# Masking the second batch on VectorE instead of TensorE, with an earlier table load, slots in three arrays and a planner that counts bank turns, in a fused attention and MoE kernel

## The chip, the cores and the metric

The kernel runs on one core of one Trainium2 chip. The metric is the device time of one execution in microseconds. A run's profile gives the span from the first to the last instruction; the time of the profiled execution is about 2 us more than its span.

## What is computed

Local attention with two kinds of masks, then a two-layer network with a leaky ReLU, all in fp32 at the interface:

```python
B, H, S, D = 8, 8, 576, 64
scores = q @ k.T / sqrt(D)
rel = pos[:, None] - pos[None, :]
mask_plain = (rel >= 0) & (rel < 32)                      # heads 0 to 3
mask_dil = (rel >= 0) & (rel < 128) & (rel % 4 == 0)      # heads 4 to 7
attn = softmax(where(mask, scores, -1e9))
x = (attn @ v).transpose(0, 2, 1, 3).reshape(B * S, H * D)   # 4608 x 512
h = x @ w_in                                              # 512 x 2048
out = maximum(0.01 * h, h) @ w_out                        # 2048 x 512
```

## The kernel before

**Attention.** The batches are taken one after another (`attend`). Each batch has four visits, in the order 2, 3, 0, 1; visits 2 and 3 are the dilated heads (`dil`), 0 and 1 the plain ones, two heads a visit, and each visit has two units. For a visit, q and k are cast to fp16 (`nat`), turned so that the head dimension lies across partitions, and stored with v in one of six slots, which lie side by side in one SBUF array `slots`: q, k and v of slot 0, then those of slot 1, and so on. For batches 0 and 1 (`b < EARLY`, EARLY = 2) the turning is done by TensorE into a PSUM bank (`tp`, and for batch 0 also others), from which VectorE or ScalarE copy into the slot (lines 398 and 400); the last 64 rows of q and k come by `load_rest` and `turn_rest` through the tile `rest`. Later batches are turned on VectorE.

A unit (`unit`) makes the scores of 384 or 416 columns with five matmuls in one PSUM bank (`p_bank`, line 775), takes exponentials on ScalarE into an fp16 tile `ee` (line 782), and then uses `ee` twice on TensorE: sums over keys (line 793 or 810), and products with v (line 793). ScalarE turns the sums into reciprocals by a logarithm and an exponential (lines 818 and 820, tile `rc`), and VectorE multiplies them into the products and writes `xt` (line 831).

Masking is done in two ways. For batches 0 and 1 (`by_pe`), two or three matmuls with the identity write a bias of 0 or -60000 into the bank ahead of the scores (line 771); the bias lies in the small part of the constants, loaded first. From batch 2 on, VectorE multiplies the exponentials in `ee` by a table of zeros and ones (line 786); the table is the large part of the constants, 400 KB.

**The network.** `up` multiplies `xt` by w_in into PSUM (lines 850 and 879), ScalarE applies the leaky ReLU on the way to `gt` (lines 865 and 891). For the first four output tiles `down` multiplies by w_out directly, in four parts of which the last needs the last pieces of w_out (line 916). Later tiles go in groups of four with seven block products in place of eight (line 1006), for which VectorE prepares sums (lines 946 and 992). The last three chunks use the same scheme for w_in (line 1275), with scratch memory in the slots that attention no longer needs.

**What sets the order.** Every piece of work is a task with candidate engines, an estimated cost, and dependencies. `_Plan` simulates the engines, chooses engine and order, repeats this nine times with priorities taken from the result, and keeps the shortest plan; the kernel is then issued in that order, one in-order queue to each engine. Margins (`MARGIN`) stretch the estimates of an engine after the planned time `CALM`. The loads of batches 0 and 1 and of the weights are in a fixed order, the list `FIRST`: q, v, r (the rest of q and k) with batch and head group, w0 to w7 for w_in, w8 to w15 for w_out, c for the table, and "." for a further piece of a v load. All of these but a few are issued from SyncE. The weights come as fp32 into tiles not yet used for anything else (`gt`, `wst`, `xt`), and VectorE and GpSimd cast them (line 387).

A rule of the framework adds semaphores where two engines use the same PSUM bank or overlapping memory.

Of the kernel before, what the change touches and what calls it, by code (L numbers as in the profile page):

```python
# [10 lines left out]
FP32 = mybir.dt.float32  # L11
# [41 lines left out]
class _Task:  # L53
    __slots__ = ("choices", "eng", "lat", "deps", "fn", "prio", "soft", "n", "start", "done",
                 "dur", "left", "ready", "users", "service", "kind", "late", "fixed", "rows", "yields")

    def __init__(self, choices, lat, deps, fn, prio, soft, n, kind):
# [10 lines left out]
        self.yields = []  # L68


class _Plan:
# [22 lines left out]
    def forward(self):  # L94
# [14 lines left out]
        cached = {}  # L109
        while len(order) < len(self.tasks):  # L110
            best = None
            for eng, cand in waiting.items():
# [4 lines left out]
                else:  # L117
# [10 lines left out]
                    for t in cand:  # L128
                        if len(t.choices) > 1:
                            end = max(here, t.ready) + dict(t.choices)[eng] * _margin(eng, here)  # L130
                            if any(max(free.get(e, 0.0), t.ready) + d * _margin(e, here) < end - 0.02
                                   for e, d in t.choices if e != eng):
                                continue
# [3 lines left out]
                    else:  # L137
                        at = max(here, min(t.ready for t in could))
                        pick = min(((t.ready + t.soft > at + 1e-9, t.prio, t.n), t)
                                   for t in could if t.ready <= at + 1e-9)  # L140
# [124 lines left out]
def kernel(  # L265
# [51 lines left out]
    KB, VB, TS = S, 3 * S, 5 * S  # L317
# [3 lines left out]
    slots = sbuf("slots", [128, NT * TS])  # L321
# [58 lines left out]
    def cast(dst, src, n, deps, prio, engines=("POOL", "DVE"), slow=1.0):  # L380
        cost = {"POOL": 0.15 + n * 0.00102 * slow, "DVE": 0.07 + n * (0.00055 if slow == 1.0 else 0.0011),
# [12 lines left out]
    def move(dst, src, n, deps, prio, eng=("DVE",), dense=False):  # L394
# [8 lines left out]
        return add(tuple((e, cost[e]) for e in eng), None, 0.2, deps, fn, prio)  # L403
# [18 lines left out]
    def clear_slots(which, prio, deps):  # L422
        for i in which:
            t_zero[i] = [clear((("DVE", 0.62), ("POOL", 0.7)),
                               slots[:, i * TS + x:i * TS + x + 2 * S].bitcast(FP32), None, 0.0,
                               prio + 0.01 * i, deps) for x in (KB, VB)]
# [6 lines left out]
    def slot(i, x, p0, p1, *dims):  # L433
        return at(slots, p0, p1, i * TS + x, *dims)
# [1023 lines left out]
```

## Time and profile before

| | us |
|---|---|
| median of 3 runs | 298.97 |
| lowest and highest | 298.3, 300.19 |
| profiled execution | 299.48 |
| its span | 297.5 |

The page's first part gives busy time by engine, the second the busy tenths in 40 slices of 7.4 us. PE is the matmuls and PEld the weight loads beside them; DVE is VectorE, ACT ScalarE, POOL GpSimd, SP SyncE. L786 is line 786 of the kernel. Matmuls are pipelined: the duration of one in the trace includes an end that lies under the next, so that a group of matmuls is better read from the chain of waits, which gives each step's own share of the time. Where a view names what ended an idle time, it is the semaphore that came last.

### The profile page before, as it was taken

Reading aid. Unit: us, or ns where it says so; the run is one execution under the profiler, and the core shown is the slowest. Engines: PE = TensorE matmul, PEld = TensorE weight load, DVE = VectorE, ACT = ScalarE, POOL = GpSimd, SP = SyncE. Lnnn points to the kernel's source line nnn. Section 1 sums busy time; section 2 is a strip of 40 time slices with the busy share of each in tenths; the row PEclk is TensorE's granted clock in tenths of the full one; section 3 lists DMA queues with packets and bytes.
Section 4 is the critical chain, followed back from the end, with each engine's and each line's share of the span. In section 5 each row is a group of like instructions: output and inputs, shape, how many; then the busy total and the mean of one; then the engine's idle time right before and its main releaser. Section 6 shows DMA issues by size and latency. Waiting matters only on the chain.

```text
span 297.5 us, 7792 instructions
## 1 busy us (share of the span) xinstructions
PE 284.5 (96%) x2975; PEld 225.4 (76%) x2975; DVE 218.1 (73%) x406; ACT 218.5 (73%) x502; POOL 144.0 (48%) x201
## 2 busy tenths in 40 slices
PE   5788989999999999999999999999999999999995
PEld 2665666678667788777777787776789999999984
DVE  6784375975689979738768869999757786587742
ACT  1797469678988884778878876886877787877611
POOL 5545555197778766776885759997100100000000
PEclk9999999999999999999999999999999999999999
DMA  7999999989988989988997998670101210111033
GB/s 216 325 303 402 322 356 249 140 165 169 155 181 175 210 187 149 231 164 173 205 150 197 166 211 160 145 211 3 36 16 53 79 36 2 37 71 39 35 108 106
DMA packets 155973, 47.16 MB, mean 159 GB/s; under 512 B 136736, under 2 KB 153248, under 8 KB 155936
## 3 DMA queue, kind: packets, MB, share of 16 engines
q1 hardware_dynamic: 155248, 46.04, 65.6%
q10 hardware_dynamic: 688, 0.63, 0.7%
q8 instruction: 23, 0.38, 0.6%
q14 instruction: 14, 0.11, 0.1%
HBM read 37.22 MB, written 9.44 MB: 157 GB/s over the span
## 4 chain that ended last, share of the span: by engine, by line
PE 75%; DMA 11%; DVE 5%; SPq 4%; issue 2%; ACT 1%; POOL 1%; DVEq 0%; POOLq 0%
PE hps L850 22%; PE fps L1006 21%; PE tp L1006 8%; PE hps L1275 5%; SPq L373 4%; DMA xt<-in_moe_w_out_dram 3%; PE ops L1275 3%; DMA vst<-in_v_dram 3%; DMA wst<-in_moe_w_in_dram 3%; PE ops L793 3%; PE fps L916 3%; PE hps L879 2%; PE ops L775 2%; DMA stg<-in_k_dram 2%; PE sps L793 1%
## 5 line engine op out<-in xcount | busy, mean ns | idle before, releaser
L850 PE MATMUL hps<-xt,w_in 128*128 128x384 f16 x488 | 95.2, 325 | 1.0 <-DVE w_in L387 0.6
L1006 PEld LDWEIGHTS <-gt 128*128 128x128 f16 x768 | 72.5, 98 | 9.8 <-DVE gt L992 0.4
L865 ACT ACTIVATE gt<-hps 128x384 f16<-128x384 f32 x122 | 59.1, 490 | 20.6 <-PE hps L850 19.5
L850 PEld LDWEIGHTS <-w_in 128*128 128x128 f16 x512 | 45.8, 98 | 23.9 <-issue 1.0
L387 POOL CAST slots<-vst 64x576 f16<-64x576 f32 (+2 forms) x60 | 52.2, 880 | 13.9 <-DVE ee L786 3.9
L387 POOL CAST nat<-stg 128x576 f16<-128x576 f32 (+1 forms) x55 | 41.4, 771 | 20.6 <-PE ops L793 6.8
L1006 PE MATMUL fps<-w_out,gt 128*128 128x256 f16 x368 | 47.0, 272 | 0.0
L786 DVE TENSOR_TENSOR ee<-ee,con 128x384 f16<-128x384 f16 (+1 forms) x48 | 22.2, 464 | 15.5 <-ACT ee L782 15.2
L820 ACT ACTIVATE rc<-rc 128x288 f32<-128x288 f32 x64 | 27.9, 442 | 0.9
L831 DVE TENSOR_TENSOR xt<-ops,rc 128x288 f16<-128x288 f32 x40 | 17.9, 448 | 11.9 <-ACT rc L820 7.7
L775 PEld LDWEIGHTS <-slots 128*128 128x128 f16 x320 | 18.4, 97 | 5.6 <-DVE slots L400 0.9
L400 POOL COPY slots<-turned 64x64 f16<-64x64 f16 (+2 forms) x36 | 19.2, 540 | 6.6 <-DVE turned L619 3.4
L793 PEld LDWEIGHTS <-slots 128*128 128x128 f16 x320 | 17.7, 97 | 4.9 <-issue 1.6
L1035 ACT COPY stg<-fps 128x512 f32<-128x512 f32 (+1 forms) x24 | 12.8, 531 | 11.1 <-PE fps L1006 10.4
L782 ACT ACTIVATE ee<-ops 128x384 f16<-128x384 f32 (+1 forms) x39 | 19.5, 503 | 1.7 <-PE ops L775 0.8
L398 ACT COPY slots<-turned 64x512 f16<-64x512 f16 (+1 forms) x28 | 18.6, 663 | 1.9 <-DVE turned L619 1.5
L818 ACT ACTIVATE rc<-ops 128x288 f32<-128x288 f32 x39 | 15.7, 408 | 5.7 <-PE ops L810 2.8
L802 POOL TENSOR_TENSOR ee<-ee 128x128 f16<-128x128 f16 x9 | 5.4, 601 | 29.2 <-DVE ee L786 29.2
L1302 ACT ACTIVATE gt<-slots 128x384 f16<-128x384 f32 x36 | 18.3, 526 | 0.9 <-DVE slots L1295 0.7
L619 DVE STREAM_TRANSPOSE turned<-nat 128x576 f16<-128x576 f16 x24 | 18.0, 761 | 0.1
L992 DVE TENSOR_TENSOR gt<-gt 128x1024 f16<-128x1024 f16 x21 | 17.1, 819 | 0.4 <-PE fps L1006 0.2
L1275 PEld LDWEIGHTS <-stg 128*128 128x128 f16 x192 | 16.3, 98 | 0.3
(137 smaller groups left out, 554.1 us busy)
## 6 DMA issues: line engine op xcount, KB each, us to landing
out_dram<-osb SPq DMA_DIRECT2D x32, 256.0 KB, 2.7
stg<-in_q_dram SPq DMA_DIRECT2D x48, 144.0 KB, 3.4
stg<-in_k_dram SPq DMA_DIRECT2D x48, 144.0 KB, 3.5
vst<-in_v_dram SPq DMA_DIRECT2D x14, 288.0 KB, 4.2
gt<-in_moe_w_in_dram SPq DMA_DIRECT2D x6, 512.0 KB, 7.1
vst<-in_v_dram SPq DMA_DIRECT2D x24, 128.0 KB, 3.0
stg<-in_q_dram SPq DMA_DIRECT2D x3, 512.0 KB, 9.7
stg<-in_k_dram SPq DMA_DIRECT2D x3, 512.0 KB, 9.5
```

The costliest lines, as they stand in the source:

```text
L387: return ENG[e].tensor_copy(out=dst, in_=src)
L398: nc.scalar.copy(out=dst, in_=src)
L400: ENG[e].tensor_copy(out=dst, in_=src)
L775: nc.tensor.matmul(p_bank[:, c:c + w], slot(tn, KB + 128 * s, 0, 128, [1, 128]), slot(tn, qx, 0, 128, *qd), start=first or not by_pe, stop ...
L782: lambda e: nc.scalar.activation(out=et[:, 0:n], in_=p_bank[:, 0:n], func=AF.Exp, scale=SCALE), prio)
L786: lambda e: nc.vector.tensor_tensor(out=et[:, 0:n], in0=et[:, 0:n], in1=con[:, table:table + n], op=ALU.mult), prio,
L793: nc.tensor.matmul(at(dst, 0, 128, o, *od), lhs(s), et[:, c:c + w], start=i == 0, stop=i == len(steps) - 1, skip_group_check=True)
L820: lambda e: nc.scalar.activation(out=rt, in_=rt, func=AF.Exp, scale=-1.0), prio)
L850: nc.tensor.matmul(ht[:, 0:n], at(w_in, 0, 128, vi * DFF + j // 2 * 256 + j % 2, [2, 128]), at(xt[m % 2], 0, 128, vi * 1152 + x0 + x, [1, n]),
L865: lambda e: nc.scalar.activation(out=gt[c % NG][:, j * n_c + x:j * n_c + x + n], in_=ht[:, 0:n], func=AF.Prelu, alpha=0.01),
L1006: nc.tensor.matmul(bk[:, x:x + HN], tl[:, off + j * step:off + j * step + 128], rhs(j), start=first and x == 0 and j == 0, stop=j == HJ - ...
L1275: nc.tensor.matmul(b[:, i * HT:i * HT + HT], lhs(v, j0 + i), rhs(v), start=first and i == 0 and v == 0, stop=i == 1 and v == 1, skip_group ...
```

## The change

1. `by_pe` holds for batch 0 alone. In batch 1 the exponentials are written back to the score bank in fp32, and VectorE multiplies them there by the table into the fp16 tile.
2. In `FIRST` the table (c) stands ahead of r1 and v11 and no longer last.
3. `slots` becomes three arrays, `q_in`, `k_in` and `v_of`. The scratch pieces of the last chunks lie in the k and v arrays.
4. In the plan, a copy out of a shared PSUM bank can't begin before the other engine's use of that bank is done.
5. Some candidates for engines change: casts of the first loads and of the rest go to VectorE or ScalarE, a small copy of k to GpSimd or ScalarE. VectorE's casts are estimated at 0.76 ns a column and not 0.55.
6. The margins, `CALM`, `WHEN` and `LATE` have other values; loads before `CALM` have a margin of 1.06.

```diff
-ROOM, LATE = 256, 0.5
+ROOM, LATE = 256, 1.5
-WHEN = (0.0, 0.0, 40.0, 70.0, 100.0, 125.0, 150.0, 180.0)
+WHEN = (0.0, 0.0, 40.0, 72.2, 97.4, 125.0, 150.0, 179.6)
-MARGIN = {'ACT': 1.02, 'DVE': 1.062, 'POOL': 1.0, 'PE': 1.0, 'SP': 1.0, 'DMA': 1.133, 'LAND': 1.15}
-CALM = 38.8
+MARGIN = {'LOAD': 1.06, 'ACT': 1.02, 'DVE': 1.023, 'POOL': 1.0, 'PE': 1.037, 'SP': 1.0, 'DMA': 1.133, 'LAND': 1.15}
+CALM = 38.5
...
-    return MARGIN[name] if at > CALM else 1.0
-FIRST = ('r0 q01 v01 . q00 w0 v00 . w1 w2 w3 w4 w5 w6 w7 w8 w9 w10 q11 w11 r1 v11 . w12 '
-         'w13 q10 v10 w14 . w15 . . c')
+    return MARGIN[name] if at > CALM else MARGIN['LOAD'] if name == 'DMA' else 1.0
+FIRST = ('r0 q01 v01 . q00 w0 v00 . w1 w2 w3 w4 w5 w6 w7 w8 w9 w10 q11 w11 c r1 v11 . '
+         'w12 w13 q10 v10 w14 . w15 . .')
...
+        cached, bank_at = {}, {}
+
+        def when(t, eng):
+            who, done = bank_at.get(t.bank, (eng, 0.0))
+            return t.ready if who == eng or t.bank is None else max(t.ready, done)
...
+            if t.bank is not None:
+                bank_at[t.bank] = (eng, t.done)
+                touched.update(("ACT", "DVE"))
...
-    KB, VB, TS = S, 3 * S, 5 * S
+    KB, VB, KS = S, 3 * S, 2 * S
...
-    slots = sbuf("slots", [128, NT * TS])
+    q_in = sbuf("q_in", [128, NT * S])
+    k_in = sbuf("k_in", [128, NT * KS])
+    v_of = sbuf("v_of", [128, NT * KS])
...
-        cost = {"POOL": 0.15 + n * 0.00102 * slow, "DVE": 0.07 + n * (0.00055 if slow == 1.0 else 0.0011),
+        cost = {"POOL": 0.15 + n * 0.00102 * slow, "DVE": 0.07 + n * (0.00076 if slow == 1.0 else 0.0011),
...
-                             ("POOL", "DVE", "ACT") if first else ("POOL", "DVE"))
+                             (("DVE", "ACT") if g else ("POOL", "DVE", "ACT")) if first else ("POOL", "DVE"))
...
-                       at(st, 0, 64, o * 512 + 256 * g, [64, 2], [128, 2], [1, D]), 256, [lo] + r_old, prio)
+                       at(st, 0, 64, o * 512 + 256 * g, [64, 2], [128, 2], [1, D]), 256, [lo] + r_old, prio,
+                       ("POOL", "DVE") if b else ("DVE", "ACT"))
...
-                                    at(xk, p0, p1, 512, [1, D]), 64, [tk] + old, prio, ("POOL", "DVE")))
+                                    at(xk, p0, p1, 512, [1, D]), 64, [tk] + old, prio, ("POOL", "ACT")))
...
-                       512, after_q + old, prio, ("DVE", "ACT"), True)]
+                       512, after_q + old, prio, ("DVE", "ACT"), True, key(tpb))]
...
-        by_pe = b < EARLY
+        by_pe, there = b < 1, b == 1
...
-        t_e = add("ACT", 0.06 + n * 0.00085, 0.22, [t_s] + e_old,
-                  lambda e: nc.scalar.activation(out=et[:, 0:n], in_=p_bank[:, 0:n], func=AF.Exp,
+        to = p_bank if there else et
+        t_e = add("ACT", 0.06 + n * 0.00085, 0.22, [t_s] + ([] if there else e_old),
+                  lambda e: nc.scalar.activation(out=to[:, 0:n], in_=p_bank[:, 0:n], func=AF.Exp,
                                                  scale=SCALE), prio)
         t_m = t_e if by_pe else add(
-            "DVE", 0.45, 0.15, [t_e, t_con[0]],
-            lambda e: nc.vector.tensor_tensor(out=et[:, 0:n], in0=et[:, 0:n],
+            "DVE", 0.56 if there else 0.45, 0.2 if there else 0.15, [t_e, t_con[0]] + (e_old if there else []),
+            lambda e: nc.vector.tensor_tensor(out=et[:, 0:n], in0=to[:, 0:n],
                                               in1=con[:, table:table + n], op=ALU.mult), prio,
-            0.0, "m")
+            0.0, "M" if there else "m")
...
-        tn = (u_tail[1] + i // 3) % NT
+        x = ((-(-u_tail[1] * KS // 768) + i // 2) % 9) * 768
...
-        return slots[:, tn * TS:tn * TS + 2304].bitcast(FP32)[:, i % 3 * 384:i % 3 * 384 + 384], old, users
+        return (k_in, v_of)[i % 2][:, x:x + 768].bitcast(FP32), old, users
```

More of the change, by code (lines that the diff above doesn't have):

```diff
@@ L54 @@
     __slots__ = ("choices", "eng", "lat", "deps", "fn", "prio", "soft", "n", "start", "done",
-                 "dur", "left", "ready", "users", "service", "kind", "late", "fixed", "rows", "yields")
+                 "dur", "left", "ready", "users", "service", "kind", "late", "fixed", "rows", "yields", "bank")
     def __init__(self, choices, lat, deps, fn, prio, soft, n, kind):
@@ L68, in __init__ @@
         self.yields = []
+        self.bank = None
 class _Plan:
@@ L129, in forward @@
                         if len(t.choices) > 1:
-                            end = max(here, t.ready) + dict(t.choices)[eng] * _margin(eng, here)
-                            if any(max(free.get(e, 0.0), t.ready) + d * _margin(e, here) < end - 0.02
+                            end = max(here, when(t, eng)) + dict(t.choices)[eng] * _margin(eng, here)
+                            if any(max(free.get(e, 0.0), when(t, e)) + d * _margin(e, here) < end - 0.02
                                    for e, d in t.choices if e != eng):
@@ L137, in forward @@
                     else:
-                        at = max(here, min(t.ready for t in could))
-                        pick = min(((t.ready + t.soft > at + 1e-9, t.prio, t.n), t)
-                                   for t in could if t.ready <= at + 1e-9)
+                        at = max(here, min(when(t, eng) for t in could))
+                        pick = min(((when(t, eng) + t.soft > at + 1e-9, t.prio, t.n), t)
+                                   for t in could if when(t, eng) <= at + 1e-9)
                         got = (at, pick[1].n, pick[1])
@@ L402, in move @@
                 "POOL": 0.24 + n * 0.001}
-        return add(tuple((e, cost[e]) for e in eng), None, 0.2, deps, fn, prio)
+        t = add(tuple((e, cost[e]) for e in eng), None, 0.2, deps, fn, prio)
+        t.bank = bank
+        return t
     rings = {}
@@ L690, in turn_rest @@
         c, r_users = raw[b, "rest"]
-        t_old, t_users = grab(hps[1] if b == 0 else tpb)
+        held = hps[1] if b == 0 else tpb
+        t_old, t_users = grab(held)
         bk = hps[1].bitcast(FP16) if b == 0 else tpb
```

30 lines of the change are left out of this document (15 added, 15 removed).

## The prediction

> **What bounds the kernel now.** I read the page's busy times and slices first, then a table of stretches, then the chain of work that ended last.
>
> ```profile
> PE 284.5 (96%) x2975; PEld 225.4 (76%) x2975; DVE 218.1 (73%) x406; ACT 218.5 (73%) x502; POOL 144.0 (48%) x201
> PE   5788989999999999999999999999999999999995
> DMA  7999999989988989988997998670101210111033
> ```
>
> TensorE is filled after the first 8 or so slices of 7.4 us. The stretches say how well (columns: length, then busy us of PE, PEld, DVE, ACT and POOL with their instructions, the granted clock, the DMA share, GB/s):
>
> ```profile
> 20.00:30.00 10.00, 9.01 (x87) 5.78 (x87) 5.27 (x12) 7.64 (x20) 5.32 (x8) 1.00 1.00 385
> 35.00:40.00 5.00, 3.60 (x43) 2.75 (x41) 2.81 (x8) 1.85 (x4) 1.60 (x3) 1.00 1.11 316
> 40.00:45.00 5.00, 5.00 (x67) 4.22 (x66) 4.10 (x11) 4.14 (x12) 3.29 (x7) 1.00 1.08 357
> 45.00:50.00 5.00, 4.98 (x64) 3.55 (x63) 2.53 (x6) 4.73 (x13) 2.89 (x4) 1.00 1.13 264
> 50.00:60.00 10.00, 9.91 (x115) 6.23 (x115) 9.02 (x15) 6.95 (x17) 1.98 (x4) 1.00 0.94 155
> 60.00:80.00 20.00, 20.00 (x217) 15.33 (x216) 13.21 (x25) 16.99 (x40) 17.16 (x24) 1.00 0.88 160
> 80.00:90.00 10.00, 9.22 (x92) 6.36 (x91) 8.52 (x15) 9.04 (x23) 7.08 (x11) 1.00 0.87 179
> 200.00:210.00 10.00, 9.62 (x88) 7.05 (x86) 10.00 (x18) 7.31 (x18) 6.89 (x8) 1.00 0.16 55
> ```
>
> The clock is 1.00 throughout, so only work and waiting count. From 40 us on TensorE has no idle time to speak of, except 0.78 us (80 to 90) and 0.38 us (200 to 210). Before that it idles 0.99 us (20 to 30) and 1.40 us (35 to 40), while the DMA share is at or above 1.00. There are therefore two stages: loading, in which DMA sets the pace, and a long stage in which each microsecond of TensorE work is a microsecond of the kernel. The chain of waits shows where the first hands over:
>
> ```profile
> 41.55 9.59 DMA xt<-in_moe_w_out_dram
> 51.19 0.88 POOL w_out L387
> 52.11 0.38 PE fps L916
> ...
> 53.74 0.18 PE ops L771 x3
> ...
> 54.11 0.18 PE hps L771 x2
> ```
>
> The last piece of w_out (step w15) is issued at 41.55, cast by 52.07, and its matmul begins at 52.11. All weights lie ahead of that point. So what ends the load stage is the landing of w15, and what TensorE could do beside it.
>
> **The change part by part.** The profiled run took 299.48 us, 1.98 more than its span, and 0.51 more than the median of 298.97. I sum on 299.48 and take off 0.51 at the end.
>
> *Mask matmuls of batch 1 go.* Its 8 units had two or three L771 matmuls each, half of the 44 weight loads that line has for batches 0 and 1; the last group of them in the timeline:
>
> ```profile
> L771 PEld LDWEIGHTS <-con x44: 95/98/99, 9.9 to 56.7; 128*128 128x128 f16 x44
> ```
>
> ```profile
> 56.70 0.34 PE L771 MATMUL sps<-con 128*128 128x64 f16 x3
> ```
>
> The chain gives 0.18 us of TensorE for either count (the timeline's 0.34 holds the last one's pipelined end). 8 x 0.18 = 1.44 us. Three groups lie behind the landing of w15, so 3 x 0.18 = 0.54 us is gained even if TensorE waits for w15; the other 0.90 only if it doesn't.
>
> *The mask on VectorE.* No VectorE instruction here multiplies exponentials in PSUM by the table. Nearest rows (busy us, mean ns of one; then, by tile, ns min/median/max):
>
> ```profile
> L1295 DVE TENSOR_TENSOR slots<-hps,slots 128x384 f32<-128x384 f32 x16 | 8.9, 554 | 5.0 <-PE hps L1275 4.1 <-ACT slots L1287 0.6
> L786 DVE TENSOR_TENSOR ee<-ee,con 128x384 f16<-128x384 f16 x24 | 11.4, 479 | 9.0 <-ACT ee L782 8.8
> L1043 DVE TENSOR_TENSOR osb<-tp,stg 128x512 f32<-128x512 f32 x14 | 9.6, 686 | 4.2 <-PE tp L1006 2.5 <-ACT stg L1035 1.5
> L782 ACT ACTIVATE ee<-ops 128x416 f16<-128x416 f32 x19 | 9.8, 517 | 1.2 <-DVE gt L992 0.5 <-PE ops L775 0.4
> L786 DVE TENSOR_TENSOR ee<-ee,con x48: 321/374/939, 66.8 to 234.2; 128x384 f16<-128x384 f16 x24, 128x416 f16<-128x416 f16 x24
> L625 POOL COPY slots<-turned x12: 694/707/1661, 63.0 to 198.8; 128x576 f16<-128x576 f16 x12
> ```
>
> L1295 has one operand in PSUM, 384 columns, 554 ns; L1043 gives (686-554)/128 = 1.03 ns for each further column, so 587 for 416. Four units of each: 4.6 us. From below, the SBUF mask L786 at its 374 ns median gives 3.0; I take 4.6, as the operand in PSUM is what the new instruction shares with L1295. It adds VectorE time and lengthens each unit's way from scores to sums. VectorE was busy 4.10+2.53+9.02 = 15.65 us of 40 to 60, so 4.35 is free there: on average it just doesn't fit (0.25 over). But copies out of PSUM may go to ScalarE (15.82 of 20 busy) and casts to GpSimd (8.16). What waits behind a mask on VectorE's queue are the copies of q and k out of the transpose bank and the xt products. I charge nothing in the likeliest case; the charge is the second rival. ScalarE's exponential, now written to PSUM in fp32, I leave at L782's 517 ns; no row shows that write, and even 0.1 us more or less on 8 of them is below 1 us on an engine with 4 free.
>
> The row shows L786 between 321 and 939 ns, and L625 on GpSimd between 694 and 1661: these lengthen each other or something third lengthens both. If the new masks had that cost too, 8 x (939-321) = 4.9 us would be lost on VectorE or GpSimd beside the casts of w_out. The Trainium skill (SBUF — State Buffer, "Who interferes with whom") says that a VectorE instruction with two SBUF inputs contends with a GpSimd instruction that reads SBUF, and one with at most one SBUF input doesn't. By that rule a mask read from PSUM would add none of the 4.9; no run shown so far can confirm it.
>
> *The table, 11 steps earlier.*
>
> ```profile
> con<-consts SPq DMA_DIRECT2D x1, 400.0 KB, 8.1
> 45.76 1.61 SPq L373 DMA_DIRECT2D con<-consts  x1
> ```
>
> It moves ahead of r1, v11, w12, w13, q10, v10, w14 and w15, all on SyncE's queue, and pushes each back. 400 KB at the 385 GB/s of 20 to 30 is 1.06 us, at the 264 of 45 to 50 1.55. Against that, the slow 264 is the stretch in which the table's packets themselves came along with the tail of w15: at the 357 of the stretch before, the same 1.32 MB would take 3.70 us and not 5. If half of those 1.3 us comes back to w15, its landing moves by 0.4; ends 0 and 1.55. I take 0.3 on the path in the likeliest case.
>
> *Slots as three arrays, bank turns counted, list anew.* What they can win are waits between in-order queues. In the timeline (start, length, engine, line, in brackets the idle time before and who ended it) and in the list of waits (sum, count, longest):
>
> ```profile
> 37.04 0.41 DVE L400 COPY slots<-tp 64x512 f16<-64x512 f16 x1
> 37.49 0.58 ACT L398 COPY slots<-tp 128x512 f16<-128x512 f16 x1 [1.82 <-DVE slots L400]
> 38.10 0.43 DVE L400 COPY slots<-tp 64x512 f16<-64x512 f16 x1 [0.65 <-ACT slots L398]
> 38.90 0.82 PE L879 MATMUL hps<-xt,w_in 128*128 128x192 f16 x8 [1.41 <-ACT gt L891]
> ```
>
> ```profile
> ACT slots L398 <- DVE slots L400: 4.6, 7, 1.8
> POOL slots L387 <- DVE slots L400: 1.7, 1, 1.7
> ```
>
> Copies by two engines from one bank (tp) follow each other, never overlap. The planner doesn't know that yet: ScalarE stood 1.82 us in front of such a copy, its Prelu came late, and TensorE waited 1.41. With bank turns in the plan this stall should go: -1.40. The second wait is a v cast held by a copy of q or k into the same large array; separate arrays part these. With the first casts off GpSimd,
>
> ```profile
> 6.52 0.29 DVE L387 CAST rest<-stg 64x256 f16<-64x256 f32 x1 [1.69 <-DMA stg<-in_k_dram]
> 6.55 0.85 POOL L387 CAST rest<-stg 64x256 f16<-64x256 f32 x1 [2.52 <-DMA stg<-in_k_dram]
> ```
>
> (0.85 against 0.29 us) I give them half of the 0.99 us idle at 20 to 30: -0.50. Of the late 0.78 + 0.38 = 1.16 us half, as a new list may close these stalls or open others: -0.58. Bounds of these three together: -3.55 (all idle time named) and, where the list opens as much as it closes, 0.
>
> *Sum*: -1.44 + 0.3 - 1.40 - 0.50 - 0.58 = -3.62, so 295.86, less 0.51: **295.4 us**. It needs TensorE to have other work at hand while w15 lands 0.3 us later.
>
> **The rivals.** *One: the landing of w15 sets the end whatever comes before.* For it: the chain runs straight through it, and q, k and v of batch 1's plain heads arrive behind the table as well, so idle time won before 52 us has nothing to be filled with. Against it: TensorE was busy 4.98 of 5 us just before, so it did have work. Then the gains before 52 us don't count: +1.06 - 0.54 - 0.58 = -0.06, that is 298.9.
>
> *Two, the other sign: batch 1's attention ends too late because of the masks.*
>
> ```profile
> 59.55 2.75 PE L916 MATMUL fps<-w_out,gt 128*128 128x512 f16 x12
> 60.48 0.46 DVE L831 TENSOR_TENSOR xt<-ops,rc 128x288 f16<-128x288 f32 x1 [0.94 <-ACT rc L820]
> 62.14 1.48 PE L879 MATMUL hps<-xt,w_in 128*128 128x192 f16 x16
> ```
>
> Its last xt product ends at 60.94, and TensorE turns to matmuls that need it at 62.14, having just used up L916: 1.20 us of slack. The table takes 1.06 of it, so the masks decide from 0.14 us on. For it: VectorE is 9.02 of 10 busy in 50 to 60, and each mask stands between a score and everything later. Against it: the weight sums in that stretch can slide. If three quarters of the 4.6 us fall on that path: 3.45 + 1.06 - 1.20 = +3.31, that is 302.8, less 0.51: 302.3. The matmuls saved don't help here, since TensorE would be waiting.
>
> *Three: the list gains nothing on balance.* Masks gone, table at its full price, stalls as before in sum: -1.44 + 1.06 = -0.38, so 298.6.
>
> **How the numbers follow.** The bound is 1% of 298.97, 2.99 us (about what a measurement of this kernel can tell from no change): faster below 295.98, slower above 301.96. My case has 0.54, with its own range from 294.0 (-1.44 and all 3.55 us of idle time) to 296.8 (the list's 20 to 30 and late terms at nought, and 0.3 more for the table); three quarters of it, 0.41, lies below 295.98. Rival one 0.18, rival three 0.08, both within 1%. Rival two 0.20, of which 0.17 is above 301.96 and the rest, with fewer masks on the path, within. So 0.41 faster, 0.42 the same, 0.17 slower. The range of 294.0 to 301.5 leaves out rival two's upper part (0.17) and 0.03 below.
>
> **What would show it.** Right: 22 L771 matmuls less; 8 VectorE products near 554 to 587 ns from PSUM between 40 and 60 us; w15 cast by about 52.4; TensorE busy over 4.5 us of 35 to 40; no 1.8 us wait of L398 on L400. Rival one: TensorE idle before L916 on w15's cast, which ends at 53 or later. Rival two: the last xt product of batch 1 after 62 us, and idle time of TensorE ahead of L879 or L850 put to VectorE. I would be wrong altogether if the long stage changed: a stretch between 90 and 280 us with TensorE under 9.5 of 10.

## The result, and the profile after

The kernel after takes 303.5 us (median of 4 runs, 301.75 to 304.86), the kernel before on the same chip 299.58. The ratio is 1.0139, with a 95% interval of 1.0095 to 1.0183: about 1.4% slower. The forecast was 295.4 with a range up to 301.5, so it was wrong in sign and size. Runs more than 1.5% above the fastest of their kernel count as slow, and the medians, ranges and ratios of this document are of the others.

Line numbers of the kernel after are some 10 to 16 higher than those of before: L802 is the mask, L809 the products with `ee`, L790 the scores, L408 and L396 copies and casts, L1008 the gate sums, L932 the direct products with w_out.

The profiled run of the kernel after has a span of 303.1 us, the one before 297.5, so there are 5.6 us to account for. First the page of the kernel after: busy time, then TensorE's busy tenths and granted clock in 40 slices of 7.6 us.

```profile
PE 287.8 (95%) x2952; PEld 227.9 (75%) x2952; DVE 218.4 (72%) x406; ACT 221.1 (73%) x522; POOL 141.8 (47%) x189
PE   5979997999997999999999999999999999999995
PEclk9979999599999999999999999999999999999999
```

TensorE is busier than before by 3.3 us, although the mask matmuls are gone, and its clock falls in two places. Three stretches for each kernel show where (length, then busy us of PE, PEld, DVE, ACT, POOL, the mean granted clock, the DMA share, GB/s; the last stretch ends with the span). The kernel before:

```profile
0.00:40.00 40.00, 31.44 (x318) 20.48 (x319) 24.25 (x56) 24.43 (x56) 20.87 (x36) 1.00 0.98 316
40.00:60.00 20.00, 19.88 (x243) 14.00 (x242) 15.65 (x30) 15.82 (x39) 8.16 (x13) 1.00 1.02 233
60.00:304.00 244.00, 233.18 (x2419) 190.93 (x2417) 178.19 (x320) 178.28 (x407) 114.98 (x153) 1.00 0.57 122
```

The kernel after:

```profile
0.00:40.00 40.00, 33.20 (x310) 22.81 (x311) 22.87 (x56) 25.94 (x60) 18.17 (x33) 0.96 0.97 311
40.00:60.00 20.00, 17.11 (x180) 11.48 (x179) 15.68 (x32) 14.71 (x36) 10.22 (x15) 0.83 0.98 235
60.00:304.00 244.00, 237.53 (x2468) 193.56 (x2465) 179.83 (x320) 180.44 (x427) 113.37 (x142) 1.00 0.57 123
```

Idle time is the length less PE's busy time; the time that the slow clock cost is estimated as busy time x (1 - clock).

| stretch | idle before | idle after | difference | slow clock after |
|---|---|---|---|---|
| 0 to 40 | 8.56 | 6.80 | -1.76 | 33.20 x 0.04 = 1.33 |
| 40 to 60 | 0.12 | 2.89 | +2.77 | 17.11 x 0.17 = 2.91 |
| 60 to the end | 4.32 | 5.57 | +1.25 | 0 |

With the 1.44 us of mask matmuls taken off, this makes -1.76 + 2.77 + 1.25 + 1.33 + 2.91 - 1.44 = 5.06 of the 5.6; the other 0.5 I can't place. Most of the loss of this run lies between 40 and 60 us. There the timeline of the kernel after has these waits of TensorE (start, length, engine, line, operation; in brackets the idle time and who ended it):

```profile
45.16 0.33 PE L809 MATMUL ops<-ee,con 128*128 128x96 f16 x5 [0.46 <-DVE ee L802]
49.50 0.33 PE L809 MATMUL sps<-ee,con 128*128 128x96 f16 x5 [0.17 <-DVE ee L802]
50.85 0.36 PE L790 MATMUL hps<-q_in,k_in 128*128 128x96 f16 x5 [0.84 <-ACT k_in L408]
52.95 0.50 PE L809 MATMUL hps<-ee,con 128*128 128x96 f16 x5 [0.61 <-DVE ee L802]
54.11 0.53 PE L809 MATMUL sps<-ee,v_of 128*128 128x96 f16 x5 [0.66 <-ACT v_of L396]
```

The reader should see two kinds of waits. Three end with a VectorE mask (L802): 0.46 + 0.17 + 0.61 = 1.24 us. Two end with ScalarE's copy of the last keys (L408) and its cast of last values (L396): 1.50 us. Before, no wait of any of these kinds stood here. Further on, batch 1's last product into `xt` starts at 64.72, where it had started at 60.48. TensorE does not wait for it, and is busy for all of 60 to 80:

```profile
64.72 0.46 DVE L847 TENSOR_TENSOR xt<-ops,rc 128x288 f16<-128x288 f32 x1 [0.19 <-ACT rc L836]
66.37 1.48 PE L895 MATMUL hps<-xt,w_in 128*128 128x192 f16 x16
60.00:80.00 20.00, 20.00 (x222) 15.06 (x220) 15.15 (x24) 15.42 (x38) 14.14 (x17) 1.00 0.91 166
```

And the long stage has a hole at 90 to 100, where TensorE waits for a gate sum (L1008 on VectorE):

```profile
90.00:100.00 10.00, 8.37 (x83) 6.34 (x82) 10.00 (x15) 7.55 (x20) 9.63 (x12) 1.00 1.04 222
```

```profile
92.68 1.05 PE L1022 MATMUL tp<-w_out,gt 128*128 128x256 f16 x8 [1.63 <-DVE gt L1008]
```

The clock doesn't explain the loss alone. The four runs of the kernel after had mean clocks of 0.981, 0.987, 0.994 and 1.00 and took 304.86, 304.24, 302.75 and 301.75 us: even the last is 2.2 us above the median of before. The profile is of the first, so the 1.33 + 2.91 = 4.24 us of slow clock weigh more in the sum above than in the median.

### The profile page after: what moved, and what is told of

The parts are those of the page before. It is cut to its first block, busy times and chain, and to the rows that moved or that the text cites. A ratio compares the mean times of both kernels' runs of the same rounds, so it can differ in the third digit from the quotient of the medians.

```text
span 303.1 us, 7763 instructions
## 1 busy us (share of the span) xinstructions
PE 287.8 (95%) x2952; PEld 227.9 (75%) x2952; DVE 218.4 (72%) x406; ACT 221.1 (73%) x522; POOL 141.8 (47%) x189
## 4 chain that ended last, share of the span: by engine, by line
PE 81%; DMA 8%; DVE 4%; ACT 4%; POOL 1%; issue 1%; SPq 1%; DVEq 0%
PE hps L866 22%; PE fps L1022 22%; PE tp L1022 8%; DMA vst<-in_v_dram 6%; PE hps L1291 5%; PE fps L932 4%; PE ops L809 3%; PE ops L1291 3%; PE ops L790 2%; ACT gt L881 2%; PE sps L809 2%; PE hps L895 2%; DMA stg<-in_k_dram 2%; PE sps L790 1%; PE sps L1291 1%; PE ops L1022 1%
## 5 line engine op out<-in xcount | busy, mean ns | idle before, releaser
L397 POOL CAST v_of<-vst 64x576 f16<-64x576 f32 (+2 forms) x58 | 48.7, 852 | 14.8 <-DMA vst<-in_v_dram 8.4
L802 DVE TENSOR_TENSOR ee<-ee,con 128x384 f16<-128x384 f16 (+1 forms) x48 | 23.4, 492 | 15.9 <-ACT ee L798 15.8
L410 POOL COPY k_in<-turned 64x512 f16<-64x512 f16 (+2 forms) x27 | 20.5, 761 | 9.3 <-DVE turned L633 4.7
L790 PEld LDWEIGHTS <-k_in 128*128 128x128 f16 x320 | 19.8, 102 | 6.3 <-issue 1.3
L408 ACT COPY k_in<-turned 64x64 f16<-64x64 f16 (+2 forms) x45 | 21.3, 486 | 2.9 <-DVE turned L633 2.4
L809 PEld LDWEIGHTS <-v_of 128*128 128x128 f16 x320 | 18.2, 99 | 3.9 <-ACT v_of L396 0.8
L798 ACT ACTIVATE ee<-ops 128x384 f16<-128x384 f32 (+1 forms) x36 | 17.9, 501 | 2.5 <-PE ops L790 2.4
L932 PE MATMUL fps<-w_out,gt 128*128 128x512 f16 x64 | 18.2, 418 | 0.0
L1022 PE MATMUL tp<-w_out,gt 128*128 128x256 f16 x120 | 15.6, 273 | 1.6 <-DVE gt L1008 1.6
L1008 DVE TENSOR_TENSOR gt<-gt 128x1024 f16<-128x1024 f16 x21 | 15.8, 758 | 1.2 <-PE fps L1022 1.2
```

The costliest lines, as they stand in the source:

```text
L397: return ENG[e].tensor_copy(out=dst, in_=src)
L408: nc.scalar.copy(out=dst, in_=src)
L410: ENG[e].tensor_copy(out=dst, in_=src)
L790: nc.tensor.matmul(p_bank[:, c:c + w], slot(tn, KB + 128 * s, 0, 128, [1, 128]), slot(tn, qx, 0, 128, *qd), start=first or not by_pe, stop ...
L802: lambda e: nc.vector.tensor_tensor(out=et[:, 0:n], in0=to[:, 0:n], in1=con[:, table:table + n], op=ALU.mult), prio,
L809: nc.tensor.matmul(at(dst, 0, 128, o, *od), lhs(s), et[:, c:c + w], start=i == 0, stop=i == len(steps) - 1, skip_group_check=True)
```

## The experiments

Runs of one kernel measured together differ by up to 4 us (before: 296.89 to 300.78 in one such batch, 296.89 to 301.6 over all), so a ratio is good to some 0.3 to 1%, and single profiled runs show where time goes better than how much. The theories: M, the masks on VectorE put an operation into a chain that TensorE waits for; T, the earlier table pushes the last loads back; L (later N), the order that the planner makes with the new list costs; C, the slow clock costs.

**First round: one part undone, the order planned anew.** e1 masks batch 1 on TensorE again:

```diff
-        by_pe, there = b < 1, b == 1
+        by_pe, there = b < EARLY, False
```

> The changed kernel with batch 1 masked by TensorE again (as before), the table still early. Theory M (masks on VectorE make TensorE wait between 50 and 54 us): that wait goes, the clock stays at 1.00 after 50 us, 299.5 to 300.5 us. Theory T (the table pushes w15 and the last v of batch 1 back): the landings stay late, w15 is cast after 52.3, 301.5 to 303.5. Theory L (the new list and candidates): 301.5 or more, without a wait on masks.

e2 does the same and puts c back to the end of `FIRST`, so that only arrays, bank turns, candidates and list values are new:

```diff
-FIRST = ('r0 q01 v01 . q00 w0 v00 . w1 w2 w3 w4 w5 w6 w7 w8 w9 w10 q11 w11 c r1 v11 . '
-         'w12 w13 q10 v10 w14 . w15 . .')
+FIRST = ('r0 q01 v01 . q00 w0 v00 . w1 w2 w3 w4 w5 w6 w7 w8 w9 w10 q11 w11 r1 v11 . '
+         'w12 w13 q10 v10 w14 . w15 . . c')
```

> As e1_pe_masks and the table last in the list again, so that the three arrays, bank turns, candidates and list values are all that is left of the change. Theories M and T: 298 to 300, as before or a little faster, w15 cast by 51.5. Theory L: 301.5 or more.

e3 is the kernel after with the table built on the chip from the biases that are there (an exponential on ScalarE, eleven copies on GpSimd) and not loaded:

```diff
+    t_ones = add("ACT", 0.25, 0.22, [t_id], lambda e: nc.scalar.activation(
+        out=ones, in_=con[:, M_BIAS:M_BIAS + 160], func=AF.Exp), -1700)
...
+        t = add("POOL", 0.24 + n * 0.001, 0.2, [t_ones], lambda e: nc.gpsimd.tensor_copy(
```

> The changed kernel, but the table isn't loaded: ScalarE makes 160 columns of zeros and ones from the bias by an exponential, and GpSimd copies them 11 times into the table in the first 9 us. Masks stay on VectorE. Theory T: w15 and the v pieces land 1.1 to 1.6 us earlier than in the changed kernel, 300 to 302 us. Theory M: TensorE waits for masks all the same between 49 and 54 us, 302.5 to 303.5.

e4 is the kernel after in its own order, with six idle matmuls of 512 columns in the planned gaps of TensorE between 50 and 54 us, to hold the clock:

```diff
+            w = _Task((("PE", 0.3),), 0.0, [], lambda e, b=b: nc.tensor.matmul(
+                b, warm[:, 0:128], zeros(512), start=True, stop=True), 0, 0.0, 0, "w")
```

> The changed kernel in its own order, with 6 idle matmuls of 512 columns put where the plan has TensorE idle between 50.0 and 53.5 us. Theory C (a stretch with too little TensorE work halves the granted clock for 7 us from 53 us, and that is the 3 us between the slowest and fastest of its runs): the clock stays at 1.00 from 50 to 60 us in every run, 301.2 to 302.2 us with a narrow spread. If the clock has another cause: 302 to 305, clock 0.98 to 1.00 as before.

| | median (range) us | ratio to before | idle 40 to 60 | idle after 60 |
|---|---|---|---|---|
| after | 303.5 (301.75 to 304.86) | 1.0139 [1.0095, 1.0183] | 2.89 | 5.57 |
| e1 | 303.84 (303.15 to 304.5) | 1.0137 [1.0068, 1.0207] | 1.11 | 6.63 |
| e2 | 306.75 (306.04 to 307.49) | 1.0235 [1.0164, 1.0306] | 0.28 | 9.12 |
| e3 | 303.7 (302.37 to 304.5) | 1.0128 [1.0055, 1.0201] | 2.19 | 7.08 |
| e4 | 303.47 (302.55 to 305.49) | 1.013 [1.0035, 1.0225] | 2.40 | 5.87 |

(Idle from the same kind of rows as above, each against its own span.) Without the VectorE masks the idle time at 40 to 60 falls to 1.11 and, with the table late as well, to 0.28, as before. But the time doesn't come back. In e2 it is lost later:

```profile
80.00:90.00 10.00, 7.62 (x80) 5.21 (x77) 7.93 (x14) 8.71 (x22) 5.90 (x8) 1.00 0.90 164
120.00:140.00 20.00, 17.64 (x159) 13.01 (x158) 13.85 (x22) 12.05 (x28) 10.85 (x16) 0.91 0.97 191
```

TensorE stands still for 2.38 and 2.36 us there. In e1 to e3 the planner finds another order for each edit, and a kernel with less of the change in it (e2) is slower than one with more (e1). These three therefore answer no question about a single part. e4 keeps the order, and with the clock at 1.00 from 50 to 60 it is no faster: the fall of the clock there is not the main loss. (Its 2.40 us counts the idle matmuls as work. They needn't be what held the clock: e3, without them, has 1.00 there too.)

**Second round: orders held fixed.** From here on every task keeps the engine and the place in its queue that it has in one of the two kernels, and only the part named is changed. In the old order, e5 issues the table ahead of r1:

```diff
+    t_con[0].start = before_c.start - 0.001
```

> Order of the kernel before on every engine and queue, except that the load of the mask table is issued in front of r1's (batch 1 is masked by TensorE as before). Theory T (the table's place pushes w15, and so the last values, back): slower than before by 0.5 to 1.5 us, with w15's cast past 53 us and TensorE idle 0.5 us or more at 50 to 60. Theory M (masks) and theory L (the order that the new list gives): within 0.4 us of before.

e6 masks batch 1 on VectorE from PSUM, with the table built as in e3 and not loaded (each mask stands where the plan ends its exponential):

```diff
+        w = _Task((("DVE", 0.56),), 0.0, [], fn, 0, 0.0, t.n, "M")
+        w.eng, w.start, w.dur, w.done = "DVE", t.done, 0.56, t.done + 0.56
```

> Order of the kernel before; batch 1's eight bias groups are left out and its masks put on VectorE, each at the place in VectorE's order where its exponential is planned to end; the table is built on the chip from the biases that are there, so that no load is moved. Theory M (an exponential, then a mask, then the product, with no other TensorE work at hand): slower than before by 1 to 3 us, TensorE idle 1.5 us or more at 40 to 60 against 0.11. Theory L: faster by 0.5 to 1.5 us, since 1.44 us of TensorE's work is gone and the masks find cover. Theory T: no more than 0.5 us from before.

e7 has both: these masks, and the early load of e5.

> Order of the kernel before with both edits of the mask: batch 1 masked on VectorE and the table's load in front of r1's; only the slots as arrays, the counted bank turns and the new list's values are missing against the kernel after. Theory M with T: slower than before by 2 to 4.5 us, near the kernel after. Theory L: within 1 us of before or faster, so that the whole loss is in the order made anew.

e8 has only the table built on the chip, with TensorE's masks; it is the base for e6.

> Order of the kernel before, TensorE's masks in batch 1, the table built on the chip and its load not issued. Every theory: same as before to faster by 1 us, as the rows that used to land after w15 come earlier or not; slower by 0.5 us or more if the eleven GpSimd copies get in the way of the first casts. It is the version that could beat both kernels.

In the new order, e9 brings back TensorE's bias groups in batch 1 and leaves out the eight masks, and e10 builds the table instead of loading it:

```diff
-            if by_pe:
+            if bias_on:
...
-        to = p_bank if there else et
+        to = et
```

> Order of the kernel after on every engine and queue, with batch 1's bias groups back on TensorE and its eight VectorE masks left out. Theory M: faster than the kernel after by 1.5 to 3 us (300.5 to 302), TensorE idle under 1.2 us at 40 to 60 against 2.88. Theory L: not faster, and up to 1.5 us slower, since 1.44 us of matmuls come back and the order is the same. Theory C (the clock): faster only if the clock at 53 to 59 no longer falls.

> Order of the kernel after with VectorE masks in batch 1, the table built on the chip and its load not issued, so that the last loads are issued without it. Theory T: faster than the kernel after by 0.8 to 1.5 us, w15's cast by 52 us. Theory M and theory L: within 0.5 us of the kernel after.

| | median (range) us | ratio to before | idle 40 to 60 | idle after 60 |
|---|---|---|---|---|
| e5 | 299.15 (297.64 to 300.77) | 1.0008 [0.998, 1.0037] | 1.22 | 4.22 |
| e6 | 301.63 (301.38 to 302.01) | 1.0093 [1.0064, 1.0122] | 2.91 | 4.22 |
| e7 | 302.3 (300.9 to 302.95) | 1.0104 [1.0059, 1.0149] | 2.40 | 4.29 |
| e8 | 300.43 (299.54 to 302.52) | 1.0048 [1.0019, 1.0076] | 0.35 | 4.18 |
| e9 | 303.32 (302.61 to 306.92) | 1.0175 [1.0083, 1.0267] | 2.34 | 6.44 |
| e10 | 302.52 (301.81 to 303.17) | 1.0116 [1.0063, 1.0169] | 2.12 | 5.42 |

With the early table in all four, masks and order make a square:

| | TensorE's masks | VectorE's masks |
|---|---|---|
| old order | 1.0008 (e5) | 1.0104 (e7) |
| new order | 1.0175 (e9) | 1.0139 (after) |

Theory T falls: with the early table alone the time is the same. In the new order, e10's interval without the load overlaps that of the kernel after. In e5 TensorE does wait for w15's cast,

```profile
52.59 0.85 PE L916 MATMUL fps<-w_out,gt 128*128 128x512 f16 x2 [0.83 <-DVE w_out L387]
```

but no time is lost by it that can be measured; nor is any gained from its idle time before 40 us, 6.54 us against 8.56 in the kernel before. Theory M holds in the old order: 302.3 - 299.15 = 3.15 us from e5 to e7, and 301.63 - 300.43 = 1.2 us from e8 to e6, after the 1.44 us of matmuls saved. Three of the four waits in e6 end with a mask (here L788). They stand ahead of the products with `ee`, not at the end of batch 1's attention where rival two looked for them:

```profile
47.25 0.82 PE L885 MATMUL hps<-xt,w_in 128*128 128x192 f16 x8 [0.67 <-ACT gt L897]
52.87 0.33 PE L799 MATMUL ops<-ee,con 128*128 128x96 f16 x5 [1.17 <-DVE ee L788]
55.07 0.34 PE L799 MATMUL hps<-ee,con 128*128 128x96 f16 x5 [0.17 <-DVE ee L788]
58.62 0.35 PE L799 MATMUL ops<-ee,con 128*128 128x64 f16 x5 [0.61 <-DVE ee L788]
```

Idle time at 40 to 60 goes from 0.35 (e8) to 2.91, +2.56; less 1.44 that is +1.12, and the medians differ by 1.20. This is the cleanest price of the masks. The base e8 is itself 0.5% slower than before: GpSimd builds the table ahead of the tile that TensorE's first matmuls read, and these start at 6.37 us instead of 3.05. e6 (6.23) and e10 (6.26) start as late, so e6 against e8 is a fair pair, while e10 carries the late start against the kernel after.

But theory M isn't enough. In the new order the masks can go (e9) and the kernel gets no faster. Its waits at 50 to 54 us are then these:

```profile
50.52 0.36 PE L791 MATMUL hps<-q_in,k_in 128*128 128x96 f16 x5 [0.74 <-ACT k_in L408]
53.42 0.36 PE L811 MATMUL sps<-ee,v_of 128*128 128x96 f16 x5 [1.47 <-ACT v_of L396]
```

The mask waits are gone, and the wait for the last values has grown from 0.66 to 1.47. The two causes fill the same idle time: whichever is taken away, the other is late next. That fits the square, which doesn't add up: the masks cost 1.0104 - 1.0008 = 1.0% in the old order and -0.4% in the new. With the four intervals this difference is barely clear of noise.

**Third round: single waits of the new order.** e11 moves three things at the last loads: the second of the two key copies to VectorE, the second half of w15's cast to VectorE, and w15's first product ahead of a product that waits for values. e12 makes the gate sum that the product at 92 us waits for second instead of third, and the first sum ahead of a transpose. e13 is both, e14 both with TensorE's masks.

```diff
+    moved = {470: (None, 52.63), 349: ('DVE', 49.84), 145: ('DVE', 52.25), 146: (None, 52.26), 495: (None, 88.22), 497: (None, 89.77), 496: (None, 90.57)}
+    for t in order:
+        if t.kind != "w" and t.n in moved:
+            t.eng, t.start = moved[t.n][0] or t.eng, moved[t.n][1]
```

(The first four are e11's, the last three e12's.)

> The kernel after and its order, with three moves for the end of the loads: the second of the two key copies that ScalarE makes in a row is made by VectorE; the second half of w15 is cast by VectorE beside GpSimd instead of after it; and w15's first product is put ahead of a batch 1 product that waits for the last values. VectorE masks as they are. Theory E (after the masks' own waits, the rest of the idle time at 40 to 60 is this serial work at the last landings): the 0.84 us wait for keys and the 0.66 us wait for values shrink to under 0.5 us together, idle at 40 to 60 falls from 2.88 to under 2, and the kernel is faster than the kernel after by 0.8 to 1.8 us. Theory P (the last landings hold TensorE however the work around them is ordered): the idle time moves by a microsecond or two and the time stays within 0.5 us.

> The kernel after and its order, with one move: the gate sum that the next expert product waits for is made second instead of third, and the first sum ahead of a transpose. Theory S (the stall at 90 to 100 is VectorE's order and is on the path): the 1.63 us wait for the sum shrinks to under 0.6 us and the kernel is faster than after by 0.8 to 1.6 us. Theory P: VectorE is busy all through 90 to 100, so the wait only goes to the next product and the time stays within 0.5 us.

> The kernel after with the moves at the last loads and the one at the sums. Theories E and S: 1.8 to 3.2 us faster than the kernel after, 300 to 301.5 us, not under the kernel before as the masks' own 1.24 us of waits are left. Theory P: within 0.6 us of the kernel after.

> The same moves with batch 1 masked by TensorE again. Theories E and S, with the masks' waits gone as well: 2 to 3.5 us faster than the new order with TensorE's masks, 299.5 to 301.5 us, TensorE's idle time under 1.2 us at 40 to 60 and under 1 us at 80 to 100: the two stalls are then what the order made anew cost. Theory P: within 0.6 us of the new order with TensorE's masks (303.3).

| | median (range) us | ratio to before | idle 40 to 60 | idle after 60 |
|---|---|---|---|---|
| e11 | 302.53 (301.5 to 302.64) | 1.0127 [1.0069, 1.0186] | 3.18 | 5.61 |
| e12 | 302.42 (301.16 to 304.23) | 1.0145 [1.0069, 1.0222] | 3.20 | 5.07 |
| e13 | 302.3 (300.8 to 304.67) | 1.0138 [1.0063, 1.0212] | 3.04 | 4.84 |
| e14 | 301.69 (300.26 to 302.63) | 1.0106 [1.0047, 1.0165] | 1.77 | 4.52 |

e11 misses the gain that theory E forecast. Its wait for values is gone, but the one for keys is now 1.34 and TensorE waits for w15 instead, so theory P holds for these moves:

```profile
51.13 0.36 PE L790 MATMUL hps<-q_in,k_in 128*128 128x96 f16 x5 [1.34 <-ACT k_in L408]
53.22 0.59 PE L932 MATMUL fps<-w_out,gt 128*128 128x512 f16 x2 [0.35 <-DVE w_out L397]
```

e12's wait shrinks as expected from 1.63 to 0.48:

```profile
88.88 1.05 PE L1022 MATMUL tp<-w_out,gt 128*128 128x256 f16 x8 [0.48 <-DVE gt L1008]
99.41 0.33 PE L790 MATMUL ops<-q_in,k_in 128*128 128x96 f16 x5 [0.26 <-DVE xt L847]
```

but idle time after 60 us falls by only 0.5, and no gain in time is shown. e14 has the lowest ratio in the new order; its interval overlaps that of e9, so the step is not settled either. e13, with both moves and VectorE's masks, shows no gain (1.0138).

**Fourth round: which half of the new order.** All three have the code of the kernel after (three arrays), TensorE's masks and the early table; engines and order of the tasks are set from the one or the other plan:

```diff
+        if t.n in given:
+            t.eng, t.start, t.dur = given[t.n]
+            t.done = t.start + t.dur
```

> The code of the kernel after (three slot arrays), batch 1 masked by TensorE, and every task in the order and on the engine of the old order with the table early: beside e5 only the arrays differ. Theory N (the order made anew costs, wherever it does): ratio to before within 0.4% of e5's 1.0008. Theory A (the arrays themselves cost, by other waits between engines): ratio of 1.008 or more, as a good part of e9's 1.0175.

> Same code and TensorE masks; tasks planned up to 62 us in the new order, all later ones in the old. Theory N-early (the new order loses at the end of the loads, where keys, values and w15 are waited for): ratio of 1.008 to 1.015, TensorE idle 1.5 us or more at 40 to 60. Theory N-late (it loses by the waits for gate sums and the like after 80 us): ratio of 1.000 to 1.005, the wait of 1.5 to 2 us at 90 gone.

> The reverse: old order for what is planned up to 62 us, new order for all later tasks. Theory N-early: ratio of 1.000 to 1.006. Theory N-late: ratio of 1.006 to 1.013 and the wait of 1.5 to 2 us for a gate sum near 90 us. If e16 and e17 both lie between, both parts cost, and their sum should come near e9's 1.0175.

| | order up to 62 us | order after | median (range) us | ratio to before | idle 40 to 60 | idle after 60 |
|---|---|---|---|---|---|---|
| e15 | old | old | 299.74 (298.1 to 301.38) | 1.0044 [1.0014, 1.0074] | 0.86 | 4.27 |
| e16 | new | old | 300.62 (298.37 to 302.19) | 1.007 [1.0043, 1.0098] | 2.52 | 4.26 |
| e17 | old | new | 301.83 (300.63 to 303.44) | 1.0113 [1.0078, 1.0148] | 0.36 | 5.17 |
| e9 | new | new | 303.32 (302.61 to 306.92) | 1.0175 [1.0083, 1.0267] | 2.34 | 6.44 |

The rows follow the halves: the idle time at 40 to 60 comes with the new early order, and the wait for the gate sum with the new late one. In e17 it is there again:

```profile
91.11 1.05 PE L1027 MATMUL tp<-w_out,gt 128*128 128x256 f16 x8 [1.64 <-DVE gt L1013]
```

Against e15 the late half costs 0.0113 - 0.0044 = 0.7% (2 us) and the early half 0.3% (0.8 us), the latter within its uncertainty. The idle time of the early half is thus not lost in full: 1.66 us more at 40 to 60 (2.52 - 0.86) go with 0.8 us of time. Of the late half's loss only 0.9 us is idle time after 60 us (5.17 - 4.27) in the profiled runs. The profile of e17 has 1.83 us more busy time of TensorE than that of e15 besides, and a slow clock ahead of the part that was changed (40 to 50 us, e15, then e17):

```profile
40.00:50.00 10.00, 9.64 (x126) 7.49 (x124) 7.17 (x16) 8.61 (x23) 5.62 (x10) 1.00 1.09 308
40.00:50.00 10.00, 10.00 (x110) 7.82 (x110) 6.63 (x16) 6.80 (x18) 4.80 (x10) 0.83 1.09 337
```

All six runs of e17 have a mean clock of 0.989 to 0.994, and seven of e15's eleven have 0.998 or more. The four others of e15, at 0.992 to 0.994, average 300.26 us against e17's 301.87, so some 1.6 us stay with the late order as an estimate; how much of the rest is the clock is open. The arrays differ from e5 by 0.4%, with intervals that touch, so a cost of them is not shown.

No version here beats the kernel before; e5 equals it.

## Why the prediction was wrong

**The step that failed** is the sentence "I charge nothing in the likeliest case; the charge is the second rival", said of the masks on VectorE. It takes for granted that TensorE has other work while a mask stands between the scores and the products; the condition that closes the sum, "It needs TensorE to have other work at hand while w15 lands 0.3 us later", asks this only for the landing. There was not enough. The 4.98 of 5 us busy that I read as work at hand was the work that fills those microseconds, in an order that fitted. With the masks, the old order waits 1.95 us on them in e6 (1.17 + 0.17 + 0.61). The sum had the matmuls and the masks together at -1.44 us; measured they are +1.2 (e8 to e6) to +3.15 (e5 to e7). In the kernel after the masks' own share of the waits is 1.24 us.

**The terms for arrays, bank turns and list** (-1.40, -0.50, -0.58) also failed: they were gains of 2.48 us together, and the new order is a loss (e15 to e9: 1.0044 to 1.0175). The first was right as a row: the 1.8 us wait of ScalarE on VectorE's copy is gone, and TensorE is busy throughout that stretch.

```profile
35.00:40.00 5.00, 5.00 (x51) 3.98 (x50) 2.87 (x8) 2.51 (x6) 1.68 (x3) 1.00 1.16 235
```

It was no gain, for two reasons. A new wait of 1.93 us for a cast of w_in opened ahead of 18.33 us:

```profile
18.33 0.35 PE L866 MATMUL tp<-xt,w_in 128*128 128x384 f16 x1 [1.93 <-DVE w_in L397]
```

The clock fell after it in the profiled run: of the 1.76 us less of idle time before 40 us, 1.33 are a slower clock and 0.43 a gain, where I had 1.90. And a gain before the last loads is worth little, as rival one said: e5 has 2.02 us less idle time before 40 us than the kernel before and the same time, e8 starts 3.3 us late and ends 1.4 us late, and e9 waits 2.21 us at 50 to 54 with no mask in the way. The late term had the wrong sign: the idle time after 60 us rose by 1.25 instead of falling by 0.58. By the square, the new order with TensorE's masks loses 1.7%, the masks in the old order 1.0%; their intervals overlap (0.8 to 2.7 and 0.6 to 1.5), so which is the larger is not shown.

**The table** (+0.3) costs nothing that can be measured: 1.0008 [0.998, 1.0037]. This is within its bounds of 0 and 1.55.

**The masks' own duration** was right. Of the eight, by tile:

```profile
L802 DVE TENSOR_TENSOR ee<-ops,con x3: 558/558/591, 44.5 to 57.4; 128x384 f16<-128x384 f32 x2, 128x416 f16<-128x416 f32 x1
L802 DVE TENSOR_TENSOR ee<-hps,con x3: 547/580/592, 45.0 to 59.3; 128x416 f16<-128x416 f32 x2, 128x384 f16<-128x384 f32 x1
L802 DVE TENSOR_TENSOR ee<-sps,con x2: 527/556/585, 48.9 to 61.0; 128x384 f16<-128x384 f32 x1, 128x416 f16<-128x416 f32 x1
L802 DVE TENSOR_TENSOR ee<-ee,con x48: 304/374/1964, 70.4 to 238.3; 128x384 f16<-128x384 f16 x24, 128x416 f16<-128x416 f16 x24
```

They take 527 to 592 ns. Only three of the eight run, at least in part, beside a GpSimd cast (those that start at 44.55, 52.31 and 57.35), and these, with 558, 580 and 591 ns, are no longer than the others of their size. The masks that read SBUF alone spread from 304 to 1964 in the same kernel. Of the 43 of these that stand singly in the timeline, the 24 beside no GpSimd instruction take 0.30 to 0.38 us, and 12 of the 19 beside one take 0.39 to 1.44. That agrees with the rule of the Trainium skill (SBUF — State Buffer, "Who interferes with whom"), by which an instruction with only one SBUF input stays out of GpSimd's way, though three masks are few. So the 4.9 us that the other reading would have added did not appear: the masks cost by their place in a chain, not by being lengthened.

VectorE's time at 40 to 60 did not grow by them, 15.68 us busy against 15.65. Seven of the eight lie there, but VectorE makes two copies out of the transpose bank in place of six (ScalarE 13 in place of nine) and two weight sums in place of three. Its casts did not become fewer, 6.51 us against 5.56.

**The mask matmuls** went as counted: 22 weight loads are left.

```profile
L786 PEld LDWEIGHTS <-con x22: 95/100/152, 9.3 to 22.6; 128*128 128x128 f16 x22
```

**The clock** was taken as 1.00, as it was in the profile before; that it could fall was in none of my cases. Other runs of the kernel before have mean clocks down to 0.993, but none has the 0.981 or 0.987 of the kernel after.

**The rivals.** Each shows half of its signs. For rival one w15's cast is over only at 54.87, past 53 (below), but no wait of TensorE ends with it here, as one does in e5. For rival two the last `xt` product starts at 64.72, past 62, but TensorE has no idle time ahead of L895; its waits for masks lie earlier, ahead of the products with `ee`. Rival two's 302.3 came nearest, but by a path that the trace doesn't show, which is luck, and the masks alone aren't the cause, as e9 shows. And the sign of being wrong altogether, a stretch after 90 us under 9.5 of 10, is the 8.37 above.

```profile
52.65 2.22 POOL L397 CAST w_out<-xt 128x512 f16<-128x512 f32 x2 [1.74 <-DMA xt<-in_moe_w_out_dram]
53.23 0.83 ACT L396 CAST v_of<-vst 64x576 f16<-64x576 f32 x1 [0.96 <-DMA vst<-in_v_dram]
```

Open remain: how the new late order loses the part of its 2 us that is not idle time, how much of that is the clock, and whether any hand-made repair of it pays.

## What to carry to other kernels

Taking work off the bound engine puts the replacement into a chain; charge the replacement up to its full length unless you can name, row by row, what the bound engine does in the meantime at that place. Here eight masks of 4.5 us in all took back the 1.44 us saved and 1.2 to 3.2 us more. A nearly full engine is no sign of spare work. Where a planner makes the order anew with each edit, hold the order fixed and undo one part at a time in both orders, since two causes that fill the same idle time hide one another.

## What the runs showed of the hardware

In some runs the granted clock of TensorE halves after pauses of under 2 us. One-microsecond stretches of the kernel after (length, PE busy, ..., clock) around its first fall:

```profile
16.00:17.00 1.00, 0.41 (x5) 0.13 (x2) 0.91 (x2) 1.00 (x4) 0.01 (x1) 1.00 0.67 199
17.00:18.00 1.00, 0.00 (x0) 0.00 (x0) 1.00 (x3) 0.96 (x3) 0.82 (x1) 1.00 0.92 373
18.00:19.00 1.00, 0.67 (x6) 0.60 (x7) 0.97 (x3) 0.73 (x1) 0.27 (x1) 0.76 0.77 307
...
21.00:22.00 1.00, 1.00 (x17) 0.98 (x16) 0.00 (x0) 0.95 (x4) 0.49 (x1) 0.53 1.00 377
```

and around its second:

```profile
49.00:50.00 1.00, 0.83 (x20) 0.65 (x17) 0.81 (x3) 0.96 (x2) 0.00 (x0) 1.00 1.12 280
50.00:51.00 1.00, 0.16 (x5) 0.15 (x5) 0.67 (x2) 0.99 (x3) 0.87 (x1) 1.00 1.16 208
51.00:52.00 1.00, 0.85 (x19) 0.73 (x17) 1.00 (x3) 1.00 (x4) 0.00 (x0) 1.00 0.99 182
52.00:53.00 1.00, 0.39 (x12) 0.30 (x9) 1.00 (x3) 0.27 (x1) 0.35 (x1) 0.83 0.53 95
53.00:54.00 1.00, 0.45 (x5) 0.29 (x4) 1.00 (x2) 0.78 (x1) 1.00 (x2) 0.50 0.98 155
...
58.00:59.00 1.00, 1.00 (x8) 0.53 (x7) 0.56 (x1) 0.22 (x1) 0.00 (x0) 0.50 0.37 52
59.00:60.00 1.00, 1.00 (x8) 0.49 (x7) 0.81 (x3) 0.28 (x1) 0.00 (x0) 0.76 0.34 57
```

The first fall follows a single wait of 1.93 us. The second comes within 52 to 53, with no wait over 0.84 us, after four microseconds (49 to 53) in which TensorE was busy for 2.23, and the clock stays at 0.50 for the six from 53 to 59. The Trainium skill (TensorE: Matmul & The Clock Gate, "What's actually happening") has the clock fall after an idle window of about 3.4 us and rise after a busy one, with windows that run freely. The first rise fits that length: it comes within the microsecond that ends at 22, about 3.6 us after TensorE took up work at 18.33. The second rise comes later: within 59 to 60, some five microseconds after the last wait ended at 54.11. The falls don't agree with it: neither pause was as long as 3.4 us, and a thin stretch was enough. Nor does a pause of that length always do it: the wait of 1.63 us ahead of 92.68 leaves the clock of the stretch from 90 to 100 at 1.00, and so does e9's of 2.02 us at 90.54. In another run of the same kernel the mean clock was 1.00 over the whole span, so whether it falls is not in the program alone.
